# Top-k attention with an MLP: ScalarE's copies of a group's values and scores placed behind the next step's normalizations

## The chip, the cores and the metric

The kernel runs on one core of a Trainium2 chip. The metric is the device time of one execution in microseconds. Three runs of the kernel before took 1454.36, 1457.15 and 1457.56 us; the median is 1457.15. The core's engines work at the same time, each on its own list of instructions in order, and wait for each other through semaphores: TensorE (PE) multiplies matrices into PSUM, VectorE (DVE) searches the largest scores, ScalarE (ACT) copies out of PSUM and computes exponentials, GpSimd (POOL) masks, and SyncE (SP) issues the DMAs.

## The reference

For 8 batches and 8 heads, with 576 queries and keys of 64 numbers each, attention keeps the 32 largest scores of each query; a two-layer MLP follows on 4608 tokens of 512 numbers.

```python
scores = scale * np.matmul(q, k.transpose(0, 1, 3, 2))
kth = np.partition(scores, -top_k, axis=-1)[..., -top_k:-top_k + 1]
scores = np.where(scores >= kth, scores, -1000000000.0)
scores = scores - np.max(scores, axis=-1, keepdims=True)
attn = np.exp(scores)
attn = attn / (np.sum(attn, axis=-1, keepdims=True) + 1e-09)
x = np.matmul(attn, v)        # then (B,H,S,D) -> (B*S, H*D)
h = x @ w_in
g = np.maximum(0.01 * h, h)
out = g @ w_out
```

## The kernel before

**Units and steps.** The attention is cut into 144 units. A unit is 128 queries of a pair of heads (or, for the 64 queries left of each sequence, 64 queries of two pairs). The main loop takes one step s for each unit and a few more at the end, and emits the instructions of several units at different stages. An order is written out by hand: each engine executes its instructions in the order in which the loop emits them, so moving a line of Python moves instructions in that engine's list and in no other.

**What a step emits.** In step s, VectorE searches the largest scores of unit s (`top_k`, L306 to L314, cut in four slots). GpSimd masks unit s-1 (L324, L325). Unit s-2 gets its weights (`weights_of`): VectorE takes the reciprocal of the sums (`reciprocals`, L337) and ScalarE multiplies by it (`normalize`, L340, twice). ScalarE then takes the exponentials of unit s-1 (`exponents`, L328, twice) and their sums (`sums`, L333, tile `ze`), and between the two exponentials it splits the weights of unit s-2 into halves (L349), which two DMAs and a transposing DMA (L350, L354) bring back as the tile `wT`.

**Groups of values and scores.** At the end of every second step (s even, apart from two places) TensorE multiplies the weights `wT` of two units with the values (`weigh_whole`, L393, or `weigh_left`, L405). The result lies in a PSUM tile `wide`, and ScalarE copies it to `x` (`keep_values`, L417). In the same place `scores` computes the scores of the units of steps s+2 and s+3 (L235): for each of the two units a part in a tile `wide` (keys 0 to 351) and a part in the shared tile `narrow`; the four parts are emitted in the order first unit wide, first unit narrow, second unit narrow, second unit wide. ScalarE copies them to `s_sb` (L242). There are two buffers of the tile `wide`, handed out in turn, and one of `narrow`. For some units (`KEPT`) scores were computed early and lie in DRAM, and `scores` isn't called for them.

**The MLP between.** As soon as the values of a chunk of 256 tokens are complete (`attended`), its MLP is ready: TensorE computes the hidden layer (tile `ph`, L462), ScalarE applies the leaky ReLU (Prelu to `gT`, L468), TensorE multiplies by the second matrix (tile `pz`, L474), and ScalarE copies the result to `o_sb` (L483), which a DMA stores. `mlp_steps(budget)` emits pieces of it in seven slots of each step, as many as a budget allows; `slot_budget` spreads what is outstanding over the slots until the next chunk is complete. From step 42 on, every eighth step (42, 50, ... 146) completes a chunk.

Of the kernel before, what the change touches and what calls it, by code (L numbers as in the profile page):

```python
# [20 lines left out]
def kernel(  # L21
# [196 lines left out]
    def scores(us):  # L218


        narrow = ps_sc.tile([P, 2, 512], F32, name="narrow")
        ps = {}
        for k, u in enumerate(us):
            wide = ps_sc.tile([P, 2, 512], F32, name="wide", bufs=2)
            ps[u] = ((wide[:, :, 0:WIDE], 0, WIDE),
                     (narrow[:, :, k * NARROW:(k + 1) * NARROW], WIDE, S))

        order = ((us[0], 0), (us[0], 1), (us[1], 1), (us[1], 0))
        for u, part in order:
            to, k0, k1 = ps[u][part]  # L230
            for n in range(0, len(u.quarters), 4):
                for i, pi, side, r0, q0 in u.quarters[n:n + 4]:
                    qt, kt = qk_of[pi]
                    d = slice(side * D, (side + 1) * D)
                    nc.tensor.matmul(to[r0:r0 + LEFT, i, :], qt[d, q0:q0 + LEFT],  # L235
                                     kt[d, k0:k1], start=True, stop=True)
        for u in us:
            u.both = work.tile([P, 2, S], F32, name="s_sb", bufs=5)
            u.s = [u.both[:, i, :] for i in range(2)]
        for u, part in order:  # L240
            to, k0, k1 = ps[u][part]
            nc.scalar.copy(u.both[:, :, k0:k1], to)  # L242
# [271 lines left out]
    HURRY = 20  # L514
# [3 lines left out]
    MIDDLE, END = 0, 1  # L518
# [29 lines left out]
    def slot_budget(s):  # L548

        after = [at for (at, _), _ in ready_at if at >= s]  # L550
        until = after[0] if after else s
        if len(after) >= len(CHUNKS) - EARLY:
            return EARLY_SHARE
        return backlog[0] / ((until + 1 - s) * SLOTS)
# [4 lines left out]
    with tc.manual_schedule():  # L559
        last = {p: n for n, u in enumerate(steps) for p in u.pairs}  # L560
        starts = {p: n for n, u in reversed(list(enumerate(steps))) for p in u.pairs}

        to_keep = [[steps[n] for n in (a, a + 1, a + 8, a + 9)] for a in KEPT]
        early_units = {u for us in to_keep for u in us}
        to_load, to_keep = list(to_keep), [u for us in to_keep for u in us]
        assert all(len(u.pairs) == 1 for u in to_keep)

        def score_early(count):

            for _ in range(min(count, len(to_keep))):  # L570
                keep_scores(to_keep.pop(0))
                if len(to_keep) % 4 == 0 and to_load:
                    load_early(to_load.pop(0))

        def load_more(s):

            at_once = 2
            while len(v_of) < NPAIR:
                n = len(v_of)
                due = values_at(starts[n])[0]  # L580
                if n < LOADED_V:
                    load_v(n)
                elif values_at(last[n - LOADED_V])[0] > s:
                    break
                elif due > s + 2:
                    load_v(n, at_once=False)
                elif at_once:
                    load_v(n)
                    at_once -= 1
                else:  # L590
                    break
            while len(qk_of) < NPAIR:
                n = len(qk_of)
                if n < LOADED or not to_keep and n < LOADED + 3:
                    load_qk(n)
                elif not to_keep and last[n - LOADED - 3] + 8 <= s and not waiting:
                    load_qk(n, at_once=False)
                else:
                    break


        for n in range(3):
            load_weights(n)
        jobs = [round_weights(*job) for job in ROUNDED] if AS_WORDS else [iter(())] * len(ROUNDED)
        for n in range(len(jobs) + 1):
            if n == len(jobs) - 1:
                first = first_scores(steps[0])
                next(first, None)
            for job in jobs[max(n - 1, 0):n + 1][::-1]:
                next(job, None)  # L610
            if n == len(jobs) - 1:
                next(first, None)
                load_v(0)
                load_v(1)
            elif n == len(jobs):
                for _ in first_scores(steps[1]):
                    pass
            if n:
                load_weights(n + 2)
            if n >= len(jobs) - 2 and to_load:  # L620
                load_early(to_load.pop(0))
            if 0 <= n - len(jobs) + HP + 1 < HP:
                load_qk(n - len(jobs) + HP + 1)

        def weights_of(u):
            reciprocals(u)
            normalize(u, 0)
            normalize(u, 1)

        def values(*place):  # L630
            due = [u for n, u in enumerate(steps) if values_at(n) == place]
            if not due:
                return ()
            po = ps_sc.tile([P, 2, 512], F32, name="wide", bufs=2)
            if len(due[0].pairs) == 1:
                weigh_whole(due, po, FULL + [NKC - 1] if place[1] == MIDDLE else
                            [QUARTERS] + FULL if place[0] < HURRY else FULL + [QUARTERS])
                return [(due[0], po[:, :, 0:P])]
            for n, u in enumerate(due):
                weigh_left(u, po[:, :, n * LEFT:(n + 1) * LEFT])  # L640
            return [(u, po[:, :, n * LEFT:(n + 1) * LEFT]) for n, u in enumerate(due)]

        def keep(weighed, *place):
            for u, po in weighed:
                keep_values(u.pairs[0], po, u.b, u.q0)
            attended(*place)

        for s in range(len(steps) + LAG + 1):
            assert s < 7 or not to_keep
            cur, old, older, new = unit(s), unit(s - 1), unit(s - 2), ()  # L650
            if s % 2 == 0:
                new = [u for u in steps[s + 2:s + 4] if u]
            picks = top_k(cur) if cur else iter(())
            budget = slot_budget(s)

            def slot():
                next(picks, None)

            at_first = s < HURRY and s - 2 in HURRIED
            if at_first:  # L660
                weights_of(older)
            slot()
            if old:
                mask(old, 0)
                mask(old, 1)
            late = s < HURRY and not {s - 1, s - 2} & set(HURRIED)
            if older and not late and not at_first:
                weights_of(older)
            mlp_steps(budget)
            weighed = values(s, MIDDLE)  # L670
            at_once = s - 2 in HASTY or any(at == (s, MIDDLE) for at, _ in ready_at)
            if at_once:
                keep(weighed, s, MIDDLE)
            slot()
            if older and late:
                weights_of(older)
            if s - 2 in HASTY:
                transpose_in_haste(older)
            mlp_steps(budget)
            if old:  # L680
                exponents(old, 0)
            mlp_steps(budget)
            if older:
                keep_transposed(older) if s - 2 in HASTY else transpose(older, lambda: mlp_steps(budget))
            if not older or s - 2 in HASTY:
                mlp_steps(budget)
            if unit(s + 3) in early_units:
                fetch_scores(unit(s + 3))
            else:
                load_waiting()  # L690
            slot()
            slot()
            mlp_steps(budget)
            if old:
                exponents(old, 1)
                sums(old)
            mlp_steps(budget)
            if not at_once:
                keep(weighed, s, MIDDLE)
            if new and new[0] in early_units:  # L700
                new = ()
            if new and s < HURRY:
                scores(new)
            keep(values(s, END), s, END)
            if new and s >= HURRY:
                scores(new)
            score_early(EARLY_SCORES.get(s, 0))
            budget = slot_budget(s + 1)
            mlp_steps(budget)
            load_more(s)  # L710
        mlp_steps(1e9)

# [58 lines left out]
```

## Time and profile before

| | |
|---|---|
| Median of three runs | 1457.15 us |
| The profiled execution's own time | 1456.84 us |
| Its span, first to last instruction | 1454.8 us |
| Busy: TensorE, VectorE, ScalarE, GpSimd | 1395.0, 1319.3, 1100.8, 1096.9 us |
| Granted TensorE clock, mean | 0.987 |
| ScalarE waits for TensorE's values before the copies to `x` (L417) | 111.9 us in 59 waits |
| VectorE waits for ScalarE's sums before reciprocals (L337) | 34.2 us in 29 waits |
| TensorE waits for transposed weights before values (L393) | 10.8 us in 10 waits |

Busy time is the time in which an engine has an instruction at work. The ends of matmuls are modelled, so a busy TensorE is not TensorE at its peak. In the timeline, a row shows the start in us from the span's start, the duration in us, the engine, the line of the kernel, the operation, the tile written and those read, the number of instructions, and in brackets how long the engine was idle before it and who ended that. A matmul of 32-bit numbers shows as two instructions.

### The profile page before, as it was taken

The numbers are of one execution on the slowest core, as the hardware profiler recorded it, in microseconds if no ns is written. First come the engines' busy times: TensorE is split into PE (matmuls) and PEld (weight loads), VectorE is DVE, ScalarE is ACT, GpSimd is POOL, SyncE is SP. The second block draws the span as 40 slices with busy tenths as digits, with TensorE's granted clock in tenths as the row PEclk, the third lists the DMA queues.
The fourth block names the chain that finished last, engine by engine and source line by source line (L and its number), as shares of the span: only waits on it lengthen the run. The fifth ranks groups of instructions, "written<-read, shape, count | busy, mean of one in ns | idle before, by whom it ended". The sixth has DMA issues, their size and how long they took to land.

```text
span 1454.8 us, 26041 instructions
## 1 busy us (share of the span) xinstructions
PE 1395.0 (96%) x8980; PEld 902.3 (62%) x8980; DVE 1319.3 (91%) x3401; ACT 1100.8 (76%) x1984; POOL 1096.9 (75%) x744
## 2 busy tenths in 40 slices
PE   7848999999999999999999999999999999999998
PEld 2324548575757576757575767676667666666674
DVE  7999999999999999999999999999999999999500
ACT  8878888777788787777777787878778787778710
POOL 3287888888888888788887788888788888878600
PEclk9968999999999999999999999999999999999999
DMA  8967543666566645666566645666656655544610
GB/s 328 337 222 220 146 121 94 185 159 165 150 181 173 170 138 152 175 185 190 157 166 169 171 138 156 168 192 172 169 162 175 164 152 145 159 138 123 154 40 14
DMA packets 394996, 239.14 MB, mean 164 GB/s; under 512 B 334576, under 2 KB 336112, under 8 KB 392944
## 3 DMA queue, kind: packets, MB, share of 16 engines
q1 hardware_dynamic: 394864, 237.48, 58.3%
q8 instruction: 70, 1.15, 0.3%
q14 instruction: 62, 0.51, 0.1%
HBM read 55.77 MB, written 99.09 MB: 106 GB/s over the span
## 4 chain that ended last, share of the span: by engine, by line
PE 82%; DVE 7%; DMA 5%; ACT 4%; issue 1%; POOL 0%; DVEq 0%; SPq 0%; ACTq 0%; POOLq 0%
PE pz L474 31%; PE ph L462 30%; PE wide L393 10%; PE wide L235 5%; DMA wT<-apart 3%; PE narrow L235 3%; DVE tops L311 2%; DVE pairs L314 2%; PE wide L405 1%; ACT split L349 1%; DMA raw<-in_weights_dram 1%; PE ph L430 1%; DMA apart<-split 1%; ACT s_sb L340 1%; ACT s_sb L328 1%
## 5 line engine op out<-in xcount | busy, mean ns | idle before, releaser
L324 POOL TENSOR_SCALAR pen<-s_sb,tops 128x576 f32<-128x576 f32 x288 | 637.5, 2214 | 196.3 <-DVE tops L311 129.3
L311 DVE MAX8 tops<-pairs 128x8 f32<-128x288 f32 (+1 forms) x1152 | 636.1, 591 | 0.0
L474 PE MATMUL pz<-w_out,gT 128*128 128x512 f32 x1152 | 504.7, 594 | 2.4 <-ACT scale L435 2.4
L462 PE MATMUL ph<-x,w_in 128*128 128x256 f32 x2176 | 482.6, 381 | 0.0
L314 DVE MATCH_REPLACE8 pairs<-tops,pairs 128x288 f32<-128x288 f32 (+1 forms) x864 | 460.3, 538 | 0.0
L462 PEld LDWEIGHTS ph<-x,w_in 128*128 128x128 f32 x2176 | 409.5, 190 | 77.7 <-issue 23.5
L325 POOL TENSOR_TENSOR s_sb<-s_sb,pen 128x576 f32<-128x576 f32 x288 | 406.7, 1412 | 24.1
L474 PEld LDWEIGHTS pz<-w_out,gT 128*128 128x128 f32 x1152 | 216.4, 190 | 266.7 <-issue 261.1
L349 ACT COPY split<-s_sb 128x1152 uint16<-128x1152 uint16 x280 | 309.4, 1146 | 0.1
L340 ACT ACTIVATE s_sb<-s_sb,rz 128x576 f32<-128x576 f32 x288 | 207.6, 773 | 38.6 <-DVE rz L337 38.5
L328 ACT ACTIVATE s_sb<-s_sb,nbias 128x576 f32<-128x576 f32 x288 | 222.3, 772 | 5.7 <-POOL s_sb L325 5.7
L306 DVE TENSOR_TENSOR pairs<-s_sb 128x576 f32<-128x576 f32 x288 | 213.6, 780 | 9.8 <-ACT s_sb L328 0.5
L393 PE MATMUL wide<-wT,vt 128*64 128x128 f32 (+1 forms) x2560 | 158.3, 282 | 15.6 <-DMA wT<-apart 10.8
L393 PEld LDWEIGHTS wide<-wT,vt 128*64 128x64 f32 (+1 forms) x2560 | 130.4, 137 | 64.5 <-issue 39.6
L417 ACT COPY x<-wide 128x128 f32<-128x128 f32 (+1 forms) x160 | 32.2, 260 | 125.1 <-PE wide L393 111.9
L468 ACT ACTIVATE gT<-ph 128x512 f32<-128x512 f32 x136 | 80.6, 592 | 55.1 <-PE ph L462 54.9
L242 ACT COPY s_sb<-wide 128x704 f32<-128x704 f32 x130 | 98.1, 755 | 8.9 <-PE wide L235 2.9
L483 ACT COPY o_sb<-pz 128x512 f32<-128x512 f32 x36 | 21.1, 585 | 92.1 <-PE pz L474 92.1
L235 PE MATMUL wide<-kt,qt 64*64 64x352 f32 x704 | 73.2, 479 | 0.7 <-ACT s_sb L257 0.7
L242 ACT COPY s_sb<-narrow 128x448 f32<-128x448 f32 x130 | 62.9, 536 | 0.6
L314 DVE MATCH_VALUE_LOAD pairs<-tops,pairs 128x8 f32 x864 | 62.8, 73 | 0.0
L328 ACT ACTIVATION_READ_ACCUMULATOR s_sb<-s_sb,nbias 128x1 f32 x288 | 55.3, 192 | 0.0
(69 smaller groups left out, 662.2 us busy)
## 6 DMA issues: line engine op xcount, KB each, us to landing
apart<-split SPq DMA_DIRECT2D x280, 288.0 KB, 2.1
raw<-in_weights_dram SPq DMA_DIRECT2D x15, 1024.0 KB, 7.0
vt<-in_vk_dram SPq DMA_DIRECT2D x32, 320.0 KB, 3.6
out_dram<-o_sb SPq DMA_DIRECT2D x36, 256.0 KB, 3.5
kept<-gT SPq DMA_DIRECT2D x12, 576.0 KB, 3.2
s_sb<-kept SPq DMA_DIRECT2D x12, 576.0 KB, 4.9
qt<-in_qT_dram SPq DMA_DIRECT2D x20, 288.0 KB, 3.5
kt<-in_kT_dram SPq DMA_DIRECT2D x20, 288.0 KB, 3.5
```

The lines of the kernel that those rows point to most:

```text
L235: nc.tensor.matmul(to[r0:r0 + LEFT, i, :], qt[d, q0:q0 + LEFT], kt[d, k0:k1], start=True, stop=True)
L306: nc.vector.tensor_tensor(pairs[:, :, n, :], u.both[:, :, 0:HS], u.both[:, :, HS:S], op)
L311: nc.vector.max(out=u.tops[:, i, r, :], in_=rest[i])
L314: nc.vector.match_replace(out=rest[i], in_to_replace=u.tops[:, i, r, :], in_values=rest[i], imm_value=LOWEST)
L324: nc.gpsimd.tensor_scalar(pen, u.s[i], u.tops[:, i, ROUNDS - 1, 7:8], MASKED, ALU.is_lt, ALU.mult)
L325: nc.gpsimd.tensor_tensor(u.s[i], u.s[i], pen, ALU.add)
L328: nc.scalar.activation(u.s[i], u.s[i], AF.Exp, bias=u.nbias[:, i:i + 1], scale=SCALE, accum_out=u.z[:, i:i + 1])
L340: nc.scalar.activation(u.s[i], u.s[i], AF.Copy, bias=0.0, scale=u.rz[:, i:i + 1])
L349: nc.scalar.copy(split, pairs[:, :, h])
L393: nc.tensor.matmul(po[n * D:(n + 1) * D, side, 0:P], v_of[u.pairs[0]][k, at, side, :], u.wT[k, at + side * NKC if at + 1 < NKC else at, :] ...
L462: nc.tensor.matmul(ph[:, i, 0:n], w_in[c][:, f * P:(f + 1) * P], x[c][:, 0:n], start=(c == 0), stop=(c == HP - 1),)
L474: nc.tensor.matmul(pz[0:m, 0:DMODEL], gT[:, f, r0:r0 + m], w_out[f // 4][:, f % 4, :], start=(f == 0), stop=(f == NFC - 1),)
```

## The change

`scores` becomes a generator with a stop between its matmuls and its copies. At the end of a step the loop still emits the matmuls of the values and, from step 20 (`HURRY`) on, those of the scores. In an even step that doesn't complete a chunk, ScalarE's copies of both (`keep`, and the rest of `scored`) are held in `late_group`, and emitted in the next step behind `weights_of`, that is, behind the reciprocal and the two normalizations; the MLP slot that followed them moves with them. In all other steps the order is as before.

```diff
                     nc.tensor.matmul(to[r0:r0 + LEFT, i, :], qt[d, q0:q0 + LEFT],
                                      kt[d, k0:k1], start=True, stop=True)
+        yield
         for u in us:
             u.both = work.tile([P, 2, S], F32, name="s_sb", bufs=5)
...
+        late_group = None
         for s in range(len(steps) + LAG + 1):
...
             if older and not late and not at_first:
                 weights_of(older)
+            if late_group:
+                keep(*late_group[0])
+                for _ in late_group[1]:
+                    pass
+                late_group = None
+                mlp_steps(budget)
             mlp_steps(budget)
...
             if new and s < HURRY:
-                scores(new)
-            keep(values(s, END), s, END)
-            if new and s >= HURRY:
-                scores(new)
+                for _ in scores(new):
+                    pass
+            group = values(s, END), s, END
+            scored = scores(new) if new and s >= HURRY else iter(())
             score_early(EARLY_SCORES.get(s, 0))
-            budget = slot_budget(s + 1)
-            mlp_steps(budget)
+            if s < HURRY or s % 2 or any(at == (s, END) for at, _ in ready_at):
+                keep(*group)
+                for _ in scored:
+                    pass
+                budget = slot_budget(s + 1)
+                mlp_steps(budget)
+            else:
+                next(scored, None)
+                late_group = group, scored
             load_more(s)
```

## The prediction

> **What bounds the kernel now.** I read the page's totals first, then the chain that ended last, the waits, and at last the timeline of one pair of steps. Totals, and the shares of the chain:
>
> ```profile
> PE 1395.0 (96%) x8980; PEld 902.3 (62%) x8980; DVE 1319.3 (91%) x3401; ACT 1100.8 (76%) x1984; POOL 1096.9 (75%) x744
> ...
> PE 82%; DVE 7%; DMA 5%; ACT 4%; issue 1%; POOL 0%; DVEq 0%; SPq 0%; ACTq 0%; POOLq 0%
> ```
>
> TensorE sets the end: it works on for 79 us after VectorE's last instruction at 1375.7, and from 200 us on it waits for only 10.8 us in all (2.6, 3.8 and 4.4 us in three stretches, nearly all for transposed weights, `wT`). So a microsecond that TensorE stands still costs a microsecond unless it eats one of those 10.8. The waits say how the engines lean on each other:
>
> ```profile
> ACT x L417 <- PE wide L393: 111.9, 59, 4.1
> ...
> ACT s_sb L340 <- DVE rz L337: 38.5, 43, 2.7
> ...
> DVE rz L337 <- ACT ze L333: 34.2, 29, 6.0
> ```
>
> ScalarE stands before the copy of the values (`x`) for 111.9 us because TensorE is behind. That is the gap into which the change puts the normalizations (L340). Does anything need those copies early? The stretch around the values of step 84 answers. The next step's VectorE work starts with its `pairs` row at 827.38; I call the start of the values less the start of these pairs TensorE's *lag*, here 827.19 - 827.38 = -0.19:
>
> ```profile
> 827.19 2.35 PE L393 MATMUL wide<-wT,vt 128*64 128x128 f32 x40
> ...
> 827.38 1.52 DVE L306 TENSOR_TENSOR pairs<-s_sb 128x576 f32<-128x576 f32 x2
> ...
> 829.62 0.43 ACT L417 COPY x<-wide 128x128 f32<-128x128 f32 x2 [1.23 <-PE wide L393]
> ...
> 830.40 0.15 DVE L337 RECIPROCAL rz<-ze 128x2 f32<-128x2 f32 x1
> 830.70 0.77 PE L235 MATMUL wide<-kt,qt 64*64 64x352 f32 x8
> ...
> 833.06 1.43 ACT L340 ACTIVATE s_sb<-s_sb,rz 128x576 f32<-128x576 f32 x2
> 834.39 0.76 ACT L328 ACTIVATE s_sb<-s_sb,nbias 128x576 f32<-128x576 f32 x1
> ...
> 836.02 0.60 ACT L468 ACTIVATE gT<-ph 128x512 f32<-128x512 f32 x1 [0.77 <-PE ph L462]
> 836.52 2.19 ACT L349 COPY split<-s_sb 128x1152 uint16<-128x1152 uint16 x2
> ...
> 839.75 0.17 DVE L337 RECIPROCAL rz<-ze 128x2 f32<-128x2 f32 x1 [0.41 <-ACT ze L333]
> ```
>
> The values and the scores share the PSUM tile `wide`, of which there are two. Values take one, the first unit's wide scores the other, and the second unit's wide scores (the L235 row at 830.70) take the values' buffer again: they can't start before `x` is copied. Today `x` is copied at 829.62 to 830.05 and nobody waits. The reciprocal that the normalizations need comes only at 830.40.
>
> **The change, part by part.** No instruction is added or removed. VectorE's and GpSimd's orders stay; TensorE's differs in three places by two MLP rows; SP's in one (a store of `out` goes one place ahead). The copies issue no DMA. What moves is on ScalarE, in 50 even steps from 20 on that don't complete a chunk: the two normalizations now stand ahead of the `x` copies and the four score copies. In 40 of the 50 there are both values and scores, and there the buffer matters. TensorE's order being kept, a wait at the second wide scores holds all the MLP work behind it, and ScalarE's Prelus (L468) wait for that work. The MLP slot that moves with the copies is the same work in the same TensorE place, so I cost it at nothing; were a step's MLP piece late for its Prelu, that is counted below.
>
> *Step 84, worked out.* Reciprocal 830.40 plus 0.19 (244.11 against 243.93 at the same pair of rows elsewhere): normalizations start at 830.59; from their start to that of what follows, 834.39 - 833.06 = 1.33. So `x` starts at 831.92 (before: 829.62), ends 0.43 later, and with 0.15 for the signal (an estimate between 0.04, the shortest step from TensorE's end to a Prelu, and 0.3) the second wide scores start at 832.50 instead of 830.70: **TensorE stands for 1.80 us.** ScalarE goes on: from `x` through the score copies and one Prelu 3.44 (833.06 - 829.62), so the exponential (L328) starts at 835.36 and ends at 836.23. But the next Prelu needs MLP matmuls that are 1.80 late: 837.82, not 836.02. Splits and second exponential follow in the old distances, so `ze` and the reciprocal of the next step come at 841.55. VectorE's own pace would have it at 839.34 (839.75 less its wait of 0.41): it is delayed 2.21 where it was delayed 0.41. So both engines lose 1.80.
>
> *Step 86*: values and pairs being late alike, the lag is -0.21 again. The same sum with its rows before (pairs 845.62, reciprocal 3.02 later, scores 849.00): `x` at 850.15, scores at 850.73: another 1.73 for TensorE. No Prelu stands between exponential and splits here: exponential 853.59, splits 854.46, reciprocal 857.69, against 11.96 after the pairs at VectorE's own pace (839.34 - 827.38): VectorE loses 0.11. TensorE's lag behind VectorE grows by 1.62.
> *Step 88*: lag 1.15 + 1.62 = 2.77. After the pairs: the MLP output's copy ends at 4.04 (lag + 0.69 + 0.58), normalizations to 5.37, values done at 5.21, so `x` at 5.37, ended in 0.43, and the second wide scores (lag + 3.51 = 6.28) find their buffer free. TensorE loses nothing. Exponential at 8.32 (2.95 after `x`, without a Prelu), reciprocal 4.10 later at 12.42: VectorE is delayed 0.46 (not at all before).
> *Step 90* completes a chunk and keeps the old order. There the delay of VectorE is the lag less 0.16 (lags 1.50, 1.58, 1.69, 1.70 at steps 114, 90, 82, 122; delays 1.34, 1.42, 1.53, 1.54). Lag now 1.57 + 1.62 - 0.46 = 2.73, delay 2.57 against 1.42: 1.15 more.
> Then the lag is back at -0.2 and the cycle repeats. TensorE loses 1.80 + 1.73 = 3.53, VectorE 1.80 + 0.11 + 0.46 + 1.15 = 3.52: the two agree, so a **full cycle of eight steps costs 3.5 us** on 72.8 (809.82 to 882.65).
>
> *The whole run.* The cycles that begin at 52, 84, 92, 116 and 124 are full: 5 x 3.5 = 17.5. Those at 60, 68, 76, 100, 108, 132 and 140 either lack scores in a step (they were kept before) or hold one of the `wT` waits of 0.3 to 2.3, which a late TensorE swallows: about 1.5 each, 10.5. In steps 20 to 48 the values of step 20 start 1.52 before the pairs, so the stall there is 3.1. The timeline read as at step 84 at each of the ten such steps, with every lag as it was, gives 20.8 in sum; if the first stall were a lag for good, to 3.3. I take 10, a little under the middle, since a lag once made stays for some steps there: VectorE has no delays in that stretch before. Sum: **+38 us**. Against the profiled execution's own 1456.84 (span 1454.8 and 2.0 around it) that is 1495; the median of 1457.15 is within 0.3 of it, so 1495 stands.
> Ends: with all lags as before, the 40 stalls add up to 20.8 + 37.6 (the thirty from 52 on, read in the same way) = 58, so 1515. If only the first stall of each of twelve cycles counts (1.8 x 12 = 22), the early part is 3 and the `wT` waits give back 8, it is +17, so 1474.
>
> *A rule against the trace.* 1.8 us of standing may cost clock too. In the window 50 to 100 us TensorE was busy 31.4 of 50 and was granted 0.82; in 150 to 200 it stood still for 2.9 of 50 and was granted 1.00. The Trainium skill, page "TensorE: Matmul & The Clock Gate", sections "What's actually happening" and "Why this matters for your kernels", has the clock halved by an idle window of about 3.4 us, and warns of gaps over some 3 us. By the row, 1.8 of each 18 us costs no clock. By the rule, if some 26 stalls (ten early, two in each full cycle and about one in the others) tripped it and each was followed by one such window at half clock, 26 x 1.7 = 44 would be added (an estimate): 1539. I take the row, as the stalls are shorter than the rule's gap; only step 20's 3.1 comes near.
>
> **The rivals.**
> *The stalls become a lag once a cycle (1474, chance 0.13).* For it: at a lag of 1.61 (3.02 + 0.19 + 1.33 + 0.43 + 0.15 = 5.12 after the pairs, less 3.51) the scores come no sooner than the late `x`, and a stalled TensorE is later by itself. Against: step 84's late Prelu delays VectorE too, so the lag is gone at step 86.
> *Faster (1449, 0.04).* Normalizing inside the 111.9 us of gaps brings splits and `wT` forward; three quarters of the 10.8 us of TensorE's waits go, and nothing stalls. It decides from a lag of 1.61 up; before, steps 56 and 80 have that (1.94), but in most steps behind a completed chunk the lag is -0.2.
> *No change (1457, 0.03).* Gain and stall cancel, or the buffer is free in time after all. Against: the wait is on `x` itself, and `x` is behind a reciprocal that no TensorE work moves.
> *The clock falls as well (1525 and more, 0.06).* Two thirds or more of the 44 above. For it: stalls of 3.1 early; against: the window at 150 to 200.
>
> **How the numbers follow.** The stall in both first steps of a cycle has 0.74: 1495, own range 1480 to 1513. Faster, by over 0.2% (about what a measurement of this kernel can tell from no change): 0.04; within it 0.03; slower 0.93, from the stall, the lag and the clock. For 8 in 10 the range reaches to the lag case and the upper bound of stalls: 1471 to 1514.
>
> **What would show it.** Right: TensorE waiting at L235 for ScalarE's `x` some 30 times, 1.2 to 3 us each, where there is no such wait now; VectorE's waits for `ze` up from 34 to some 65 us; its last work some 38 us later; TensorE's busy time unchanged and the stretch after VectorE's end as long as before. `x`'s waits for TensorE fall below 60. Wrong, if those L235 waits are missing or number only one a cycle, if VectorE's waits for `ze` fall, or if the granted clock falls below 0.98.

## The result, and the profile after

The changed kernel takes 1493.15 us (median of four runs, 1490.57 to 1494.46), the kernel before 1456.88 (median of four beside it, 1454.36 to 1457.56). The ratio is 1.0255, with a 95% interval of 1.0236 to 1.0273: 2.6% slower. The prediction said 1495 us, with a range of 1471 to 1514. The profiled execution took 1490.57 us; its span is 1488.6 and its mean granted clock 0.985.

The totals and the shares of the chain that ended last, of the changed kernel (lines from L236 on have moved by one: L393 is now L394, L417 is L418, and so on; the matmul line L235 has not):

```profile
span 1488.6 us, 26044 instructions
...
PE 1402.4 (94%) x8980; PEld 899.9 (60%) x8980; DVE 1320.2 (89%) x3401; ACT 1092.6 (73%) x1984; POOL 1098.1 (74%) x744
...
PE 50%; DVE 30%; ACT 14%; issue 3%; DMA 2%; POOL 0%; DVEq 0%; ACTq 0%; SPq 0%; POOLq 0%
```

VectorE, ScalarE and GpSimd execute the same numbers of instructions as before, and none of them is busy for longer by more than 1.2 us; TensorE's 1402.4 us instead of 1395.0 comes up below. What has changed is the chain: TensorE's share fell from 82% to 50%, and VectorE and ScalarE hold 44% where they held 11%. No single engine sets the end alone any more; the engines hand the delay round. The waits of the changed kernel (engine, tile and line, what ended the wait: us in total, times, longest) say where:

```profile
ACT s_sb L341 <- DVE rz L338: 108.5, 75, 3.4
...
DVE rz L338 <- ACT ze L334: 66.9, 36, 7.2
...
PEld wide L235 <- ACT x L418: 44.8, 30, 3.0
...
ACT x L418 <- PE wide L394: 35.0, 28, 2.6
PE wide L235 <- ACT x L418: 32.8, 29, 2.6
...
PE wide L394 <- DMA wT<-apart: 5.4, 7, 1.5
```

The two L235 lines are new (PEld is the weight load of the same matmuls). TensorE stands 29 times before the second unit's wide scores, until ScalarE has copied `x` out of the buffer that they need. ScalarE's own standing has only moved: 111.9 us before the copies of `x` became 35.0, and 38.5 us before the normalizations became 108.5, because these now wait at the head of the queue for a reciprocal that has not come. VectorE's waits for `ze` have doubled, from 34.2 to 66.9.

The timeline of the changed kernel around the values of step 84, the stretch that the prediction worked out (start, duration, engine, line; in brackets the idle time before the row and who ended it):

```profile
845.81 2.35 PE L394 MATMUL wide<-wT,vt 128*64 128x128 f32 x40
...
846.00 1.52 DVE L307 TENSOR_TENSOR pairs<-s_sb 128x576 f32<-128x576 f32 x2
...
847.97 0.77 PE L235 MATMUL wide<-kt,qt 64*64 64x352 f32 x8
...
849.02 0.15 DVE L338 RECIPROCAL rz<-ze 128x2 f32<-128x2 f32 x1
...
849.21 1.44 ACT L341 ACTIVATE s_sb<-s_sb,rz 128x576 f32<-128x576 f32 x2 [2.19 <-DVE rz L338]
...
850.55 0.41 ACT L418 COPY x<-wide 128x128 f32<-128x128 f32 x2
...
851.01 0.82 PE L235 MATMUL wide<-kt,qt 64*64 64x352 f32 x8 [1.51 <-ACT x L418]
...
856.39 0.60 ACT L469 ACTIVATE gT<-ph 128x512 f32<-128x512 f32 x1 [2.01 <-PE ph L463]
...
856.88 2.20 ACT L350 COPY split<-s_sb 128x1152 uint16<-128x1152 uint16 x2
...
860.12 0.17 DVE L338 RECIPROCAL rz<-ze 128x2 f32<-128x2 f32 x1 [2.15 <-ACT ze L334]
```

The values were done in time, but ScalarE waited 2.19 us for the reciprocal, and `x` was copied only at 850.55. The second wide scores started 3.04 us after the first (851.01 - 847.97). In the kernel before it was 1.35 (830.70 - 829.35), so the stall is 1.69:

```profile
829.35 0.77 PE L235 MATMUL wide<-kt,qt 64*64 64x352 f32 x8
...
830.70 0.77 PE L235 MATMUL wide<-kt,qt 64*64 64x352 f32 x8
```

Everything on TensorE behind it came late too. ScalarE then stood 2.01 us for the Prelu's matmuls (L469), ahead of the splits and the second exponential, and so VectorE got its sums 2.15 us late.

One cycle, with the prediction's terms. "Lag" is the values' start less that of the next pairs row; "stall" is how much later than 1.35 us behind the first wide scores the second ones start; "delay" is what the time between the pairs rows of two steps has over the 17.72 us in which VectorE does two steps without a wait. All are in us.

| step | lag before, after | stall before, after (predicted) | VectorE's delay before, after (predicted) |
|---|---|---|---|
| 84 | -0.20, -0.20 | 0, 1.69 (1.80) | 0.51, 2.26 (2.31) |
| 86 | -0.20, -0.21 | 0, 1.59 (1.73) | 0.01, 0.00 (0.11) |
| 88 | 1.15, 2.83 | 0, 0 (0) | 0, 0.24 (0.46) |
| 90 | 1.57, 3.01 | 0, 0 (0) | 1.41, 2.23 (2.57) |

(The prediction measured step 84's delay to the reciprocal, 0.41 and 2.21; over the pairs rows the before is 0.51, and 1.80 is added to it.) From the start of the values of step 84 to that of step 92 it is 72.8 us before and 76.2 after, 3.4 more; predicted was 3.5.

One thing more has moved. The held-back MLP slot reckons its budget at another place, so pieces of the MLP are cut differently: in 26 steps a Prelu (once an output copy) stands one place earlier or later among ScalarE's exponentials and splits. Outside the steps that hold copies back, too, ScalarE's order is therefore not quite that of before. The first experiment below has all of these 26 and loses nothing, so the loss isn't theirs; for the end of a cycle they matter.

### The profile page after: what moved, and what is told of

Same layout as the page of the kernel before. It is cut to its first block, busy times and chain, and to the rows that moved or that the text cites. A ratio compares the mean times of both kernels' runs of the same rounds, so it can differ in the third digit from the quotient of the medians.

```text
span 1488.6 us, 26044 instructions
## 1 busy us (share of the span) xinstructions
PE 1402.4 (94%) x8980; PEld 899.9 (60%) x8980; DVE 1320.2 (89%) x3401; ACT 1092.6 (73%) x1984; POOL 1098.1 (74%) x744
## 3 DMA queue, kind: packets, MB, share of 16 engines
q8 instruction: 70, 1.15, 0.3%
## 4 chain that ended last, share of the span: by engine, by line
PE 50%; DVE 30%; ACT 14%; issue 3%; DMA 2%; POOL 0%; DVEq 0%; ACTq 0%; SPq 0%; POOLq 0%
PE pz L475 30%; DVE tops L312 13%; PE ph L463 10%; DVE pairs L315 10%; PE wide L394 4%; ACT split L350 4%; ACT s_sb L341 4%; PE wide L235 3%; DVE pairs L307 3%; ACT s_sb L329 2%; ACT s_sb L243 1%; PE narrow L235 1%; DMA wT<-apart 1%; DMA raw<-in_weights_dram 1%; ACT x L418 1%
## 5 line engine op out<-in xcount | busy, mean ns | idle before, releaser
L341 ACT ACTIVATE s_sb<-s_sb,rz 128x576 f32<-128x576 f32 x288 | 207.5, 770 | 108.6 <-DVE rz L338 108.5
L394 PE MATMUL wide<-wT,vt 128*64 128x128 f32 (+1 forms) x2560 | 157.5, 282 | 9.0 <-DMA wT<-apart 5.4
L394 PEld LDWEIGHTS wide<-wT,vt 128*64 128x64 f32 (+1 forms) x2560 | 130.1, 137 | 57.7 <-issue 41.9
L469 ACT ACTIVATE gT<-ph 128x512 f32<-128x512 f32 x136 | 82.0, 603 | 73.1 <-PE ph L463 73.1
L235 PE MATMUL wide<-kt,qt 64*64 64x352 f32 x704 | 74.5, 486 | 17.9 <-ACT x L418 16.9
L338 DVE RECIPROCAL rz<-ze 128x2 f32<-128x2 f32 x144 | 22.2, 154 | 67.9 <-ACT ze L334 66.9
L418 ACT COPY x<-wide 128x128 f32<-128x128 f32 (+1 forms) x160 | 31.4, 253 | 40.0 <-PE wide L394 35.0
```

What stands on the lines that cost most here:

```text
L341: nc.scalar.activation(u.s[i], u.s[i], AF.Copy, bias=0.0, scale=u.rz[:, i:i + 1])
L394: nc.tensor.matmul(po[n * D:(n + 1) * D, side, 0:P], v_of[u.pairs[0]][k, at, side, :], u.wT[k, at + side * NKC if at + 1 < NKC else at, :] ...
```

## The experiments

The theory: the slow-down is the wait for `x`, by two handovers, the buffer (TensorE stands) and the late Prelu (VectorE loses as much, so that no lag builds up which would hide the next stall). The rivals: normalizations ahead of the score copies cost something of themselves; the stall counts only once in each cycle; the early steps or the clock carry the loss. Diffs are against the changed kernel unless the text says otherwise. Every kernel computes the whole reference. The kernel before took 1456.9 to 1462.1 us in different groups of runs, so each ratio is to its runs in the same group. The expectations in us were written for a kernel before of about 1457 us; against the slower groups they are to be read by ratio.

### Only the values copied at once

```diff
             else:
+                keep(*group)
                 next(scored, None)
-                late_group = group, scored
+                late_group = ((), s, -1), scored
```

The score copies and the MLP slot stay behind the normalizations; only the copies of `x` are back in their old place.

> As the changed kernel, but the copies of the values to x stand where they stood, at the end of the step; only the four score copies and the MLP slot go behind the normalizations. Buffer theory (TensorE stands because the second wide scores take the values' PSUM buffer, and x is copied late): no wait of TensorE for x at L235, VectorE's waits for the sums back near 34 us, time 1455 to 1461. Rival (late score copies, or the moved slot, cost the time): the time stays above 1480.

Measured: 1458.94 against 1460.7 us, ratio 0.9981 (0.9969 to 0.9994). TensorE no longer waits for `x` at L235, and VectorE's waits for `ze` are 37.9 us. The same kernel again, because so small a gain was in doubt:

> The kernel with the values' copies at once, timed again beside the two others: 0.998 as before if the small gain is real, 1.000 to 1.002 if it isn't.

Measured: 1458.35 us, ratio 0.9975 (0.9965 to 0.9985). So the whole loss sits in the place of the copies of `x`; the rest of the change (the score copies, the MLP slot and the Prelus that it shifts) gains 0.2% together.

### The same order, but an earlier reciprocal

```diff
         for n, op in enumerate((ALU.max, ALU.min)):
             nc.vector.tensor_tensor(pairs[:, :, n, :], u.both[:, :, 0:HS], u.both[:, :, HS:S], op)
+        yield
...
             slot()
+            if older and late_group:
+                reciprocals(older)
+            slot()
```

ScalarE keeps the changed order. VectorE takes the reciprocal directly behind the pairs, and not a slot later (`weights_of` then leaves it out).

> As the changed kernel, but in the steps with held-back copies VectorE computes the reciprocal right behind the pairs (about 1.5 us after their start instead of 3.0). Buffer theory: x is then copied some 1.5 us sooner, a stall of 1.7 us in the first step of a cycle shrinks to 0.1 to 0.2, and the time is 1450 to 1460. Rival (a stall belongs to the order of ScalarE's copies as such, not to when the reciprocal comes): still above 1480.

Measured: 1460.56 against 1460.7 us, ratio 0.9999 (0.9989 to 1.001). The waits of this kernel (same columns; its lines are moved by one more):

```profile
DVE rz L339 <- ACT ze L335: 39.9, 31, 8.1
...
PE wide L235 <- ACT x L419: 4.2, 3, 2.1
```

Three stalls are left of 29, and VectorE's waits are nearly as short as before (39.9 us for 34.2). The changed order on ScalarE costs nothing that can be measured as soon as the reciprocal is there; the loss is a matter of the 3.02 us between the pairs and the reciprocal, as the prediction's sum had it.

### Which steps pay

Four kernels hold the copies back in one class of steps each, by the condition that chooses the old order:

```diff
-            if s < HURRY or s % 2 or any(at == (s, END) for at, _ in ready_at):
+            if s < 48 or s % 8 != 4 or any(at == (s, END) for at, _ in ready_at):
```

This is the first step behind a completed chunk (84 is one). The second has `s % 8 != 6`, the third `s % 8`, and "early only" the old condition with `s >= 50` added to it.

> The hold-back only in steps 52, 60, 68, ... 140, the first ones behind a completed chunk, where the lag is -0.2 to 0.4. Buffer theory: ten stalls of 1.5 us less the lag, 13 us in sum, and because a Prelu that ScalarE needs for the sums is as late as TensorE, VectorE is delayed as much and nothing is given back: 1467 to 1473. Rival (a stall only becomes lag and is given back in the next steps): under 1461.

> The hold-back only in steps 54, 62, 70, ... 142, the second ones of a cycle. Buffer theory: stalls of 1.5 us less the lag, 14 us in sum, of which waits for transposed weights swallow 2 to 4: ratio 1.006 to 1.009. If the costs of the parts add up: with 0.8% for the first ones, 0.1% for the lagging ones and the early part's 0.6 to 1.0% the whole is 2.5%. Rival (the second stall exists only because of the first): under 1.003.

> The hold-back only in steps 48, 56, 64, ... 144, where TensorE lags 1.0 to 1.9 us behind the pairs. Buffer theory with the lag as its measure: stalls of 0 to 0.5 us, 2.5 us in sum, against VectorE delays of 2.5 us that go there: 1455 to 1461. Rival (each hold-back with scores costs its 1.7 us wherever it stands): ten of them, 1472 to 1476. Rival (the gap before x is worth having): under 1453.

> The hold-back only in steps 20 to 48. Buffer theory as predicted: 10 us; as the trace of the changed kernel reads: 13 us, with two windows of 3.4 us at half clock in them (1.7 us each). So ratio 1.006 to 1.010. Rival (the first stall stays as lag for good): 3 us, ratio under 1.004.

| steps that hold copies back | us, and before beside it | ratio (95%) | TensorE's waits for `x` at L235 |
|---|---|---|---|
| first of a cycle | 1473.0, 1460.7 | 1.0080 (1.0059 to 1.0102) | 11.5 us, 10 times |
| second of a cycle | 1472.83, 1462.1 | 1.0075 (1.0051 to 1.0099) | 10.5 us, 9 times |
| third of a cycle | 1461.91, 1460.7 | 1.0011 (0.9996 to 1.0026) | 0.2 us, once |
| 20 to 48 | 1474.4, 1462.1 | 1.0089 (1.0060 to 1.0117) | 10.6 us, 9 times |

The excesses add up to 0.80 + 0.75 + 0.11 + 0.89 = 2.55%, the whole loss, with about half a per cent of uncertainty from their intervals (step 48 is in two of the classes). So the second step costs as much beside the first as it does alone: the first one's stall does not turn into a lag that covers the second, as the stall of 1.59 at step 86 says too; the third, with a lag of over a microsecond before it, can't be told from no change.

### MLP work in the stall

```diff
         for u, part in order:
+            if (u, part) == order[3]:
+                yield
...
             if late_group:
                 keep(*late_group[0])
+                mlp_steps(budget)
+                mlp_steps(budget)
                 for _ in late_group[1]:
                     pass
```

The second unit's wide scores, the part that needs the buffer, are emitted behind the two MLP slots that otherwise follow them (moved there, not added), so that TensorE works on while `x` is late.

> As the changed kernel, but TensorE's last score part (the second unit's wide part, which needs the values' buffer) is emitted behind the two MLP slots that otherwise follow it, so about 1.75 us of MLP work lies between. ScalarE's order stays, but for a Prelu that comes ahead of the score copies. Buffer theory: the wait is covered by work that must be done anyway, TensorE's waits for x at L235 sum to under 8 us, time within 0.4% of the kernel before (ratio 0.996 to 1.004). Rival (it is ScalarE's later copies, not TensorE's standing, that costs): ratio over 1.015.

Measured: 1475.7 against 1462.1 us, ratio 1.0093 (1.0062 to 1.0124): a miss. The waits for `x` are gone but for 0.7 us, as meant, and 1.6 of the 2.55% with them, but a new cost came. Totals, and then waits, of this kernel:

```profile
PE 1409.6 (96%) x8980; PEld 895.4 (61%) x8980; DVE 1320.6 (90%) x3401; ACT 1093.9 (74%) x1984; POOL 1096.7 (75%) x744
```

```profile
DVE rz L340 <- ACT ze L336: 48.7, 44, 7.5
...
ACT s_sb L245 <- PE wide L237: 23.3, 31, 1.7
```

TensorE is busy for 14.6 us more than before with the same 8980 matmuls, and the span is 14.8 us longer than before (1469.6 for 1454.8): its idle time has not grown. One place shows why:

```profile
982.82 2.35 PE L396 MATMUL wide<-wT,vt 128*64 128x128 f32 x40
...
986.44 1.99 PE L465 MATMUL ph<-x,w_in 128*128 128x256 f32 x8
...
988.37 0.21 PEld L237 LDWEIGHTS wide<-raw 64*64 64x64 f32 x8 [0.33 <-ACT gT L471]
988.37 0.82 PE L237 MATMUL wide<-raw 64*64 64x352 f32 x8
...
989.12 3.07 PE L465 MATMUL ph<-x,w_in 128*128 128x256 f32 x13
```

From the start of the values to that of the second MLP stretch it is 6.30 us. The same pieces without the cut make 5.97: from the values to the MLP 4.21 (831.40 - 827.19 before), and the eight MLP rows of the piece put between 8 x 0.22 = 1.76 (14.08 us for 64 at step 84). So one more change from full-array matmuls (128*128) to quarter-array ones (64*64) and back costs about 0.33 us here, and 14.6 / 40 steps gives 0.36. The row of the weight loads shows a gap of 0.33 at the extra change, and its bracket names ScalarE. It is no wait for ScalarE: in 42 of the 43 places in this trace where such scores follow MLP matmuls, the time from the start of the last MLP matmul to that of the scores is one of two numbers, 0.31 us behind the first layer's matmuls and 0.52 behind the second's. The kernel before has the same two between MLP matmuls and values that wait for nothing. A wait would vary. ScalarE for its part waits 23.3 us for the late part of the scores, and VectorE's waits for `ze` are 48.7 us for 34.2; as TensorE's idle time hasn't grown, these did not add to its time. A covered stall is not a free one.

### The Prelu behind the splits

```diff
+            held = late_group is not None
...
-            mlp_steps(budget)
+            if not held:
+                mlp_steps(budget)
             if older:
-                ... transpose(older, lambda: mlp_steps(budget))
+                ... transpose(older, lambda: mlp_steps(0 if held else budget))
+            if held and s - 2 not in HASTY:
+                mlp_steps(budget)
+            if held:
+                mlp_steps(budget)
```

The stall stays possible, but in the steps that take held-back copies the MLP slots move behind the first splits, so a late Prelu no longer stands before them. TensorE's order is the same.

> As the changed kernel, with TensorE's order untouched; in the steps that take held-back copies ScalarE's Prelu, which waits for the late MLP work, goes behind the two splits instead of ahead of them. If VectorE's delay of 2.2 us in the first step of a cycle comes from that Prelu, as predicted, it falls to some 0.6, TensorE keeps its lag, the stall at the second step falls from 1.6 to 0.3, and a full cycle costs 2.0 us instead of 3.4: ratio 1.016 to 1.020. Rival (the Prelu has no part in it): 1.024 to 1.027.

Measured: 1472.9 against 1462.1 us, ratio 1.0078 (1.0055 to 1.0101): the direction was right, the size larger than expected. The timeline of this kernel around the values of step 84:

```profile
839.14 2.41 PE L394 MATMUL wide<-wT,vt 128*64 128x128 f32 x40
...
844.35 0.82 PE L235 MATMUL wide<-kt,qt 64*64 64x352 f32 x8 [1.45 <-ACT x L418]
...
847.56 2.24 ACT L350 COPY split<-s_sb 128x1152 uint16<-128x1152 uint16 x2
...
849.72 0.60 ACT L469 ACTIVATE gT<-ph 128x512 f32<-128x512 f32 x1
...
851.34 0.17 DVE L338 RECIPROCAL rz<-ze 128x2 f32<-128x2 f32 x1
```

The stall is there (1.62), but the splits no longer wait behind the Prelu, the reciprocal has no wait in brackets, and VectorE's delay is 0.15 instead of 2.26. TensorE's lag at step 86 is then 1.91, and step 86 has no stall. The cycle takes 74.5 us (starts of the values of steps 84 and 92), 1.7 over before. TensorE waits for `x` 17 times (20.8 us), not 29. This is the prediction's rival "a lag once a cycle", made by moving the MLP slots with the Prelu: it was the late Prelu that kept it from happening.

### Two versions without the stalls, and the Prelu's place by itself

The first two put the Prelu's new place on the kernels with the values at once and with the early reciprocal. The third is the kernel before, with its own order of copies, and nothing but the Prelu's slots moved in the same steps (`held = s % 2 == 1 and s > HURRY and ...`).

> Both mends together: the values' copies at once, only the score copies behind the normalizations, and in those steps the Prelu behind the splits. No stall at L235; VectorE's waits for the sums fall from 34 to some 20 us and TensorE's waits for transposed weights from 10.8 to about 5, since the splits come earlier. TensorE bounds the rest: ratio 0.994 to 0.998. Rival (TensorE takes back nothing, as its waits come from other steps): 0.998 to 1.001.

> The early reciprocal and the Prelu behind the splits, with the changed kernel's order of copies. Stalls at L235 only in the steps before 50 (some 4 us), TensorE's waits for transposed weights some 4 us: ratio 0.995 to 1.000. Rival (early stalls and half clock cost more than the waits give back): over 1.000.

> The kernel before with its order of copies, and only the MLP slots with the Prelu moved behind the first splits in the steps that would have held-back copies. If the gain of values at once with the Prelu behind comes from the Prelu's place alone, the ratio is 0.993 to 0.997 and VectorE's waits for the exponents fall below 35 us in all. Rival: the gain needs the score copies behind the normalizations as well; then the ratio is 0.998 to 1.001.

| kernel | us, and before beside it | ratio to before (95%) |
|---|---|---|
| values at once, Prelu behind | 1453.16, 1461.3 | 0.9942 (0.9925 to 0.9959) |
| early reciprocal, Prelu behind | 1454.59, 1461.3 | 0.9956 (0.9939 to 0.9972) |
| kernel before, Prelu behind | 1453.07, 1460.39 | 0.9951 (0.9939 to 0.9963) |

All three beat the kernel before by about half a per cent, and their intervals overlap: the gain is the Prelu's place, and the order of the copies adds nothing to it that these runs can tell. Two signs expected of the first of them did not come: VectorE's waits for `ze` were 33.4 us and not some 20, TensorE's for transposed weights 7.5 and not about 5. What the trace of the third shows of the gain is small:

```profile
DVE rz L337 <- ACT ze L333: 34.2, 29, 6.5
...
PE wide L393 <- DMA wT<-apart: 8.6, 8, 2.1
```

VectorE's waits are the 34.2 us of before, and TensorE waits 2.2 us less for transposed weights. The gain by the medians is 7.3 us (1460.39 - 1453.07), but the two executions that were profiled lie only 1.4 apart: 1456.84, from the first group of runs, and 1455.46, near the longest of its six and with one window of halved clock. So these traces can't show the rest; where it comes from stays open.

It also says how the loss divides. On a kernel that has the Prelu behind the splits, the change costs 1.0078 / 0.9951 = 1.013. So of the 2.55%, about half (1.3%, give or take 0.3) is the stall alone, and the other half is the stall seen through the Prelu.

## Why the prediction was right

**The buffer.** Right. TensorE's waits at L235 were to number some 30, of 1.2 to 3 us: there were 29 matmul waits (30 of weight loads), the longest 2.6 and 3.0, but 15 of the 29 were shorter than 1.2, down to 0.41. At step 84 the stall was 1.69 for 1.80. The estimate for the signal was the difference: it took 0.05 from the end of `x` (850.96) to the scores (851.01), not 0.15. The mean of the waits is lower, 1.13 (32.8 / 29); the wait's row shows 0.18 less than the later start at step 84 (1.51 for 1.69).

**The late Prelu and the return of the lag.** Right. Step 84 delayed VectorE by 2.26, the lag at step 86 was again -0.21, the stall came a second time, and the kernel with the Prelu moved shows that it hangs on the place of this Prelu.

**The end of the cycle.** Right in sum, not in its parts. VectorE's delay was 0.24 for 0.46 at step 88 and 2.23 for 2.57 at step 90. Lag less 0.16 would have given 2.85 there. The rule itself held at such lags: step 82 of the changed kernel has a lag of 3.02 and a delay of 2.86. But behind the values of step 90 the Prelu now stands between the two splits, and no longer ahead of both; the sum had left the Prelus in their places. First the changed kernel, then the kernel before:

```profile
912.04 1.15 ACT L350 COPY split<-s_sb 128x1152 uint16<-128x1152 uint16 x1
913.08 0.61 ACT L469 ACTIVATE gT<-ph 128x512 f32<-128x512 f32 x1
913.57 1.16 ACT L350 COPY split<-s_sb 128x1152 uint16<-128x1152 uint16 x1
```

```profile
890.62 0.60 ACT L468 ACTIVATE gT<-ph 128x512 f32<-128x512 f32 x1 [0.51 <-PE ph L462]
891.12 2.20 ACT L349 COPY split<-s_sb 128x1152 uint16<-128x1152 uint16 x2
```

So 0.6 us of lag went over into step 92 (0.42 for -0.20), and the same at steps 100, 124 and 132, each behind such a Prelu.

**The whole run.** Both of its terms, the early steps and the later cycles, were mis-sized. TensorE's start of the values, changed against before, moved from -2.66 us at step 20 (before the first held-back copy had an effect) to +10.67 at step 50: 13.3 for 10. Of these, 9.3 came in two places, at the stalls of steps 20 and 40, the two with a window of half clock behind them (below). The 3.3 too little are as much as these two windows cost (3.4), which the sum had at nothing. From step 52 to step 142 it moved another 23.0, for 28. The five cycles that were called full cost 3.5, 3.4, 1.6, 3.2 and 2.9 (those from 52, 84, 92, 116 and 124), 14.5 together for 17.5, and the seven others 8.5 for 10.5. Four of the twelve, those from 92, 100, 124 and 132, begin with the lag that a shifted Prelu left; they cost 4.0 for 10, and the other eight 19.0 for 18. That the shifted Prelus are the cause of this is read from the timeline, not tested by itself. The two errors went against each other: 36.4 from step 20 on, for 38. So it is in part luck that the total came so close; that the two stalls of the cycle from 84 cost 3.4 is not. By ratio, the kernel with early steps only says 0.89% (13 us), which leaves 1.66% for the later steps.

The sum closes from the waits as well: 32.8 us of stalls, with 0.18 more for each of 29 if all are like step 84's, is 38.0 us; two windows of half clock add 3.4; TensorE's waits for transposed weights fell from 10.8 to 5.4. That makes 36.0.

**The clock.** The row was right for 27 of the 29 stalls, which left the clock as it was; the other reading (1539 us), in which some 26 stalls trip the gate, was not. The timeline of the changed kernel at the stalls of steps 20 and 40:

```profile
252.27 1.10 PE L235 MATMUL wide<-raw 64*64 64x352 f32 x8 [2.61 <-ACT x L418]
```

```profile
437.08 1.45 PE L235 MATMUL wide<-kt,qt 64*64 64x352 f32 x8 [2.42 <-ACT x L418]
```

The windows behind the stalls of steps 40 and 84 (length, busy us of PE, PEld, DVE, ACT and POOL with counts, granted clock, DMA share, GB/s):

```profile
437.00:439.00 2.00, 1.92 (x9) 0.81 (x10) 2.00 (x6) 1.94 (x5) 1.92 (x2) 0.50 0.20 39
439.00:441.00 2.00, 2.00 (x4) 0.77 (x3) 1.90 (x3) 2.00 (x4) 0.89 (x3) 0.65 1.23 263
...
851.00:853.00 2.00, 1.99 (x14) 1.31 (x15) 2.00 (x6) 2.00 (x5) 1.92 (x2) 1.00 0.83 186
```

After step 84's stall the clock stays at 1.00; after step 40's it is 0.50, and the same eight matmuls take 1.45 us instead of 0.82. The changed kernel has two such windows from 200 us on, 252.7 to 256.1 and 437.0 to 440.4, each 3.4 us long, so 1.7 us lost in each: 3.4 us in all, not 44. At step 20 the stall (2.61 and 0.18) and 1.7 make 4.49, and by 4.49 the start of the next values moved. The other 27 stalls leave TensorE idle for at most 1.51 us. The prediction had named only step 20, with 3.1, as near the gap of some 3 us that the Trainium skill warns of (page "TensorE: Matmul & The Clock Gate", section "Why this matters for your kernels"). In the run the waits at both, 2.61 and 2.42, were shorter than that and had a window all the same: here the measurement differs from the page. The mean clock of 0.985 stayed above the 0.98 that was to be the sign of the clock rival.

**TensorE's busy time** was to stay the same and did not: 1402.4 for 1395.0. The half-clock windows are 3.4 of it and the slower start behind each stall (0.82 for 0.77 us, 29 times) 1.5; the rest is no more than such totals differ between kernels with the same matmuls and hardly a stall (1394.8 to 1399.2 us in the runs before and with values at once, with and without the Prelu moved). The other signs came: `ze` waits 66.9 for "some 65", `x` waits 35.0 for "below 60", VectorE's last reciprocal 33.7 us later (1409.23 for 1375.53) where 38 was foretold, and TensorE's last matmul 75.4 us behind VectorE's end in both kernels. (The prediction's 79 us for that stretch runs to the end of the span; TensorE ends 3.8 earlier.)

**The rivals.** "No change" and "faster" fell with the 29 waits. The argument against the lag rival named the right row. "Faster" rested on filling ScalarE's gap, and the early reciprocal shows what that is worth: with 26 of the 29 stalls gone, the normalizations in the gap give a ratio of 0.9999.

## What to carry to other kernels

When an engine stands idle before a copy, that idle time is not free for work that waits for something else: ask who needs the buffer that the copy empties, and compare when the inserted work can start with when the copy could have. In a queue, follow the delay on to the next row that depends on the stalled engine (here the Prelu); here it decided whether a stall became a lag that covered the next one or came again two steps later. In this kernel, rows that depend on the late engine were better placed behind those that the chain waits for: moving the Prelu's slots gained 0.5% by itself. And a moved slot can shift other rows of the queue: compare each engine's order before and after, not only the rows that were meant to move.

## What the runs showed of the hardware that was not expected

- Half clock came behind gaps of TensorE that are shorter than 3 us, and not behind each of them. In the traces of all these kernels, from 200 us on, there are 21 gaps of 1.89 to 2.99 us in which neither a matmul nor a weight load is at work; 14 have a window of half clock behind them, 7 (that of 2.99 us among them) don't. None of the 35 gaps of 1.41 to 1.87 us has one. What decides between 1.89 and 3 us, no run here shows.
- Cutting a run of quarter-array matmuls in two with full-array matmuls between cost about 0.33 to 0.36 us for each cut, and showed in TensorE's busy time (14.6 us over the kernel), not among its matmuls' waits.
